# A sequence mixer and an MLP in one program: each y eviction on one engine, and a new hand-fixed order for every engine

## The chip, the cores and the metric

The program runs on one core of a Trainium2 chip. Its engines each work through a queue of their own: TensorE (PE, with the weight loads PEld), VectorE (DVE), ScalarE (ACT), GpSimd (POOL), and SyncE (SP), which here only issues transfers. The metric is the time of one execution on the device, in microseconds (us), lower is better.

## The reference

Two pre-normalised blocks with residuals. The first is a state-space mixer: k is convolved with four taps, multiplied by v, put through a long causal convolution along the sequence (an FFT of 4096 points in the reference) and multiplied by the normalised q. The second normalises again and runs two MLPs, the first of them with a shift of the four channel groups along the sequence.

```python
def _A_ref(q, k, v, shift_k, ssm_k, ssm_D):
    ...
    kv = k_shift * v
    kv_f = rfft(kv padded to 2S, along the sequence); kf_f = rfft(ssm_k padded to 2S)
    y = irfft(kv_f * kf_f)[:S]
    y = y + kv * ssm_D
    return q * y

x = A_q
h = x + _A_ref(_layernorm(x), A_k, A_v, A_shift_k, A_ssm_k, A_ssm_D)
n = _layernorm(h)
x1 = n + shifted(gelu(_layernorm(n) @ w1)) @ w2
h2 = h + x1 + gelu(_layernorm(x1) @ w3) @ w4
```

S is 2048, D is 512, the hidden width of the second MLP is 1792, all in bfloat16.

## The kernel before

The kernel does the long convolution as a sequence of small matrix products (a factored transform), with the 2048 positions laid out as 128 partitions by 16 tiles. Its work is first recorded as 926 operations (`Plan.add`), each with the keys it reads and writes, the engines that may do it and a cost in microseconds. None of these costs is used when the program is built: `Plan.issue` walks a string of numbers, `ISSUE`, and emits the operations in that order. Where an operation may run on more than one engine, the number carries a letter (V for DVE, A for ACT, G for POOL). So the order of every engine's queue, and the choice of engine, are fixed by `ISSUE`; each engine works strictly in that order, and waits that follow from the data are added by the framework.

Names used below, with the lines of the profile:

- Loads, all on SP: `k.0` to `k.3` (L240), `v.0` to `v.3` (L244), `h.0` to `h.3` (L249, the long filter), of 512 KB each; `q` as eight loads of 256 KB (L430), each of 64 of the 128 partitions. The statistics of four q tiles need two such loads.
- `psh` (L477): the four taps of k as 32 matmuls, `kvq` (L481, DVE) evicts them times v; eight of each (`kvq.0` to `kvq.3` for the first half of the channels, then again `kvq.0'` to `kvq.3'` for the second). `Rk` (L488): two transfers per `kvq` that bring the product to its next layout.
- `Rh` (L171 on ACT, L173 on DVE, 128x2048): the filter transposed by PE (`pt`, L502), four evictions. A first `tensor_tensor` on POOL must have added the skip term to the filter.
- Stage A: `pak` and `pah` (L518, eight matmuls each) for kv and the filter, 16 of each, evicted by `Tk` and `Th` (128x1024).
- Stage C: `pc` (L542 to L544), 32 products, evicted by `xt`; DVE multiplies the two spectra (`pr`, L674) and adds (L688, L690) in place.
- Stage G: `pg` (L744), 16, evicted by `Gs`. All of them must be done before the next stage, since the PSUM pools are exchanged there and each product of the next stage reads all of them.
- Last level: `py.0` to `py.7` (L797), each with two tiles of 512. The eviction `y` scales each of the two by a column of `rq` and adds 1 (L805 on ACT, L807 on DVE). `hs` (L812, DVE) multiplies the pair by the centred q; then statistics (L620, L621), a chain of ten small DVE operations for the reciprocal root (`rh`, L601 to L605 and L824 to L827), and the normalisation `hn` (L840 on ACT, L843 on DVE), four blocks of four tiles.
- The normalised tiles are transposed to `xT`: for blocks 0 and 1 by PE (`pt2`, L856) with an eviction on ACT, for blocks 2 and 3 by DMA transposes on SP (L900). `pw` (L868) is a product with w1 or w3, `gT` and `g2` its GELU on ACT (L872), `p2` (L945) the product with w2, evicted by `x1` (L951, DVE); `xn` is the second normalisation, `p4` (L1014) the product with w4, followed by the addition (L1019) and the stores.
- `qc` (L634 on ACT, L636 on DVE): q minus its mean, 16 tiles; `Wf'` (L173 and L588): four small copies of a table; `pv` (L880): matmuls on zeros which keep PE running.

A transfer takes one of eight completion semaphores in turn, so that the issue of one on SP waits for the landing of the eighth before it.

## Time and profile before

| | |
|---|---|
| median of 3 runs | 243.41 us (242.63 to 243.48) |
| the profiled execution | 243.34 us, of which the span from the first to the last instruction is 241.5 us |
| DVE, ACT and POOL busy | 161.0, 153.1 and 15.4 us |
| granted PE clock | 1.00 throughout |
| read from and written to memory | 13.11 MB and 2.10 MB |

The profile gives, for each engine, the instructions in order of time with the idle time ahead of them and what released it. A busy time of n instructions in a row overlaps by some 0.1 us at each boundary, so that durations of single instructions add up to more than the time from one start to the next.

### The profile page before, as it was taken

How to read it: one execution, taken by the hardware profiler on the slowest of the kernel's cores; microseconds unless marked ns; L12 is line 12 of the kernel's file. 1: busy time of each engine (PE TensorE's matmuls, PEld its weight loads, DVE VectorE, ACT ScalarE, POOL GpSimd, SP SyncE). 2: the span in 40 equal slices, each digit the busy share in tenths (PEclk: the TensorE clock that was granted, in tenths of full speed). 3: DMA queues.
4: the chain of work that ended last, by engine and by line, in shares of the span. 5: the costliest groups of instructions: out<-in, count | busy, mean ns of one | idle time of the engine just before them, and what ended most of it. 6: DMA issues, size and time to landing. Idle time of an engine off the chain costs nothing.

```text
span 241.5 us, 5031 instructions
## 1 busy us (share of the span) xinstructions
PE 224.7 (93%) x2069; PEld 147.6 (61%) x2069; DVE 161.0 (67%) x380; ACT 153.1 (63%) x205; POOL 15.4 (6%) x30
## 2 busy tenths in 40 slices
PE   8899987998899977999969999999999999999994
PEld 7899987897799864574434544444444444444454
DVE  6954999999999997999998899910440044004421
ACT  5788769999979998889657399763036204630000
POOL 2359300000000000000000000000000000000000
PEclk9999999999999999999999999999999999999999
DMA  6998876740000099100640025320002012001111
GB/s 218 391 374 203 168 187 213 174 91 3 0 3 0 20 343 390 39 0 0 88 84 5 1 53 99 61 52 3 10 22 54 0 24 65 0 0 42 46 43 45
DMA packets 22182, 21.82 MB, mean 90 GB/s; under 512 B 11916, under 2 KB 18704, under 8 KB 22160
## 3 DMA queue, kind: packets, MB, share of 16 engines
q1 hardware_dynamic: 21904, 21.37, 32.7%
q8 instruction: 16, 0.26, 0.5%
q10 hardware_dynamic: 256, 0.14, 0.2%
q14 instruction: 6, 0.05, 0.1%
HBM read 13.11 MB, written 2.10 MB: 63 GB/s over the span
## 4 chain that ended last, share of the span: by engine, by line
PE 51%; DVE 25%; DMA 12%; ACT 6%; issue 2%; SPq 1%; DVEq 0%; ACTq 0%
PE pw L868 23%; PE p L1014 20%; DVE kin L674 6%; DMA kin<-in_A_v_dram 5%; PE p L945 4%; DVE bst L620 4%; DVE ab L173 4%; ACT s L171 3%; DMA q_sb<-in_A_q_dram 3%; ACT ab L171 3%; DMA kin<-in_A_k_dram 2%; DVE ab L812 2%; DMA act<-ab 2%; DVE kin L688 1%; DVE bst L624 1%
## 5 line engine op out<-in xcount | busy, mean ns | idle before, releaser
L868 PE MATMUL pw<-act,wts 128*128 128x512 bf16 x288 | 64.0, 379 | 2.5 <-DMA act<-ab 1.9
L872 ACT ACTIVATE ab<-pw 128x512 bf16<-128x512 f32 x56 | 33.0, 596 | 38.4 <-PE pw L868 27.3
L1019 DVE TENSOR_TENSOR wts<-p,wts 128x1024 bf16<-128x1024 f32 (+2 forms) x10 | 10.1, 1012 | 62.0 <-PE p L1014 62.0
L868 PEld LDWEIGHTS <-wts 128*128 128x128 bf16 x288 | 28.0, 98 | 36.3 <-DMA act<-ab 2.4
L1014 PE MATMUL p<-wts,ab 128*128 128x512 bf16 (+1 forms) x238 | 48.9, 366 | 0.0
L1014 PEld LDWEIGHTS <-ab 128*128 128x128 bf16 x238 | 23.3, 98 | 25.3
L542 PE MATMUL pc<-ab,Wc 128*128 128x256 bf16 x128 | 30.7, 282 | 1.4 <-DVE ab L173 1.1
L171 ACT CAST s<-pc 128x1024 bf16<-128x1024 f32 x31 | 29.6, 1044 | 1.4 <-DVE kin L674 1.3
L544 PE MATMUL pc<-ab,Wc 128*128 128x128 bf16 x128 | 29.0, 227 | 0.0
L543 PE MATMUL pc<-ab,Wc 128*128 128x128 bf16 x128 | 28.0, 219 | 0.0
L543 PEld LDWEIGHTS <-Wc 128*128 128x128 bf16 x128 | 19.4, 151 | 1.4 <-issue 1.4
L674 DVE TENSOR_TENSOR kin<-s 128x2048 bf16<-128x2048 bf16 x16 | 19.4, 1221 | 0.6
L542 PEld LDWEIGHTS <-Wc 128*128 128x128 bf16 x128 | 19.4, 151 | 0.3
L544 PEld LDWEIGHTS <-Wc 128*128 128x128 bf16 x128 | 18.2, 142 | 0.0
L477 PE MATMUL psh<-ab 128*128 128x128 bf16 x256 | 15.6, 219 | 0.4 <-DVE kvq L481 0.4
L171 ACT CAST ab<-pah 128x1024 bf16<-128x1024 f32 x13 | 12.8, 1023 | 4.8 <-PE pah L518 4.8
L477 PEld LDWEIGHTS <-ab 128*128 128x128 bf16 x256 | 14.4, 98 | 0.9 <-issue 0.4
L945 PE MATMUL p<-wts,act 128*128 128x512 bf16 x64 | 15.0, 379 | 0.0
L481 DVE TENSOR_TENSOR kvq<-psh,kin 128x1024 bf16<-128x1024 f32 x8 | 9.7, 1218 | 4.8 <-DMA kin<-in_A_v_dram 4.8
L171 ACT CAST ab<-pak 128x1024 bf16<-128x1024 f32 x13 | 12.5, 1061 | 0.0
L951 DVE SCALAR_TENSOR_TENSOR s<-ab,rho,p 128x512 bf16<-128x512 bf16 x16 | 11.5, 739 | 1.2 <-PE p L945 1.1
L1000 DVE SCALAR_TENSOR_TENSOR wts<-s,mq,ab 128x512 f32<-128x512 bf16 x16 | 11.2, 749 | 0.2
(139 smaller groups left out, 316.3 us busy)
## 6 DMA issues: line engine op xcount, KB each, us to landing
wts<-in_B_w_dram SPq DMA_DIRECT2D x2, 1792.0 KB, 11.1
kin<-in_A_k_dram SPq DMA_DIRECT2D x4, 512.0 KB, 5.8
ab<-in_A_ssm_k_dram SPq DMA_DIRECT2D x4, 512.0 KB, 8.6
kin<-in_A_v_dram SPq DMA_DIRECT2D x4, 512.0 KB, 13.6
q_sb<-in_A_q_dram SPq DMA_DIRECT2D x8, 256.0 KB, 6.1
kin<-kvq SPq DMA_DIRECT2D x16, 128.0 KB, 5.1
out_dram<-wts SPq DMA_DIRECT2D x14, 128.0 KB, 2.3
Wc<-ab SPq DMA_DIRECT2D x4, 384.0 KB, 5.3
```

The source lines that it names most:

```text
L171: A.copy(o, src)
L477: T_.matmul(pv[:, g, i, :], lhsT=row(g, 4 * qr + i - j), rhs=dg()[:, 2 * g + cc, j, :], start=(j == 0), stop=(j == 3))
L542: T_.matmul(pv[:, kk], lhsT=W[0], rhs=T[:, :, 2 * k1:2 * k1 + 2, :], start=True, stop=False)
L543: T_.matmul(pv[:, kk, :, 0, :], lhsT=W[1], rhs=T[:, :, 2 * k1 + 1, :], start=False, stop=False)
L544: T_.matmul(pv[:, kk, :, 1, :], lhsT=W[2], rhs=T[:, :, 2 * k1, :], start=False, stop=True)
L674: v(1.13, lambda: V.tensor_tensor(out=prs(), in0=xs(0).unsqueeze(1).to_broadcast([P, 2, 2, 512]), in1=xs(1).unsqueeze(2).to_broadcast([P, ...
L868: T_.matmul(ps[:], lhsT=wt(w)[:, k, m * P:(m + 1) * P], rhs=xT()[:, k, 4 * b * P:(4 * b + 4) * P], start=(k == 0), stop=(k == DC - 1))
L872: add({"A": 0.49}, lambda: A.activation(dst(), X[pkey][:], ACT.Gelu_apprx_tanh), r + [pkey, "gelu"], [key])
L945: T_.matmul(ps[:, i, :], lhsT=gT()[:, m, t + i + 2 + off[m], :], rhs=wt("w2")[:, m, :], start=(m == 0), stop=(m == 3))
L951: v(0.66, lambda t=t, i=i, key=key: V.scalar_tensor_tensor(out=qn()[:, t + i, :], in0=hn()[:, t + i, :], scalar=rho[:, t + i:t + i + 1], i ...
L1000: v(0.66, lambda j=j, i=i, t=t + i: V.scalar_tensor_tensor(out=ofb()[:, j, i], in0=qn()[:, t, :], scalar=mq[:, t:t + 1], in1=hs()[:, t, :] ...
L1014: T_.matmul(ps[:, i, x0:x1], lhsT=g2(b % 2)[:, m, s0:s0 + P], rhs=wt("w4")[:, m, x0:x1], start=(m == 0), stop=(m == FC - 1))
```

## The change

Two things change in the code. First, the two halves of a y eviction, which were two operations with an engine each, become one operation on one engine; the key `("y", u % 4, i)` becomes `("y", u % 4)`. Second, several costs of the plan are altered (small DVE operations from 0.08 to 0.14, for example), and `ISSUE` is replaced as a whole. As the costs are not read when the program is built, all that reaches the chip is the new order, the new choice of engines and the pairing.

```diff
 ISSUE = """
-19 89 91 4 87 78 1 0 2 30 92 31 22 5 20 33 88 23 7 6 8 25 12 32 24 34V 42 35 41 40 43 48 93 10 26 90 28 29 95 15
...
+2 30 19 3 23 32 87 92 31 93 24 0 5 4 41 89 40 94 42 7 91 43 6 33 48 21 22 25 27 78 90 45 46 95 44 10 20 12 47
...
 """
...
             for i, f in enumerate(fns):
-                v(0.08, f, r if i == 0 else (), w, lat=0.24)
+                v(0.14, f, r if i == 0 else (), w, lat=0.22)
...
-        add({"A": 0.71, "V": 0.325}, centre, [("mq", t // 4), ("bst", t)], [("qc", t)])
+        add({"A": 0.69, "V": 0.27}, centre, [("mq", t // 4), ("bst", t)], [("qc", t)])
...
-        for i in range(2):
-            def scaled(e, i=i, t=2 * u + i):
+
+        def scaled(e):
+            for i in range(2):
+                t = 2 * u + i
                 if e == "A":
                     A.activation(ysb()[:, u % 4, i], X[key][:, i], ACT.Identity, bias=1.0, scale=rq[:, t:t + 1])
                 else:
                     V.tensor_scalar(ysb()[:, u % 4, i], X[key][:, i], rq[:, t:t + 1], 1.0, op0=MUL, op1=ADD)
-            add({"A": 0.53, "V": 0.6}, scaled, ["W", key, ("rq", 0)], [("y", u % 4, i)])
+
+        add({"A": 1.18, "V": 1.22}, scaled, ["W", key, ("rq", 0)], [("y", u % 4)])
```

Read from the two strings, the operations that changed their engine are:

| operation | before, DVE / ACT | after, DVE / ACT |
|---|---|---|
| `Rh` | 2 / 2 | 1 / 3 |
| `Th` and `Tk` | 3 / 13 each | 4 / 12 each |
| `Gs` | 6 / 10 | 5 / 11 |
| `Wf'` | 4 / 0 | 2 / 2 |
| `y` in halves | 1 / 15 | 2 / 14 |
| `hn` | 8 / 8 | 4 / 12 |
| `xn` | 4 / 12 | 6 / 10 |
| first step of one phase table (128x1024) | on DVE | on POOL |

The order on SP of the first transfers:

```
before: k3 k0 k2 k1 h2 h0 v0 h3 h1 v1 v2 q q v3 Rk Rk q q Rk Rk ...
after:  k3 k1 k2 k0 h0 h2 h1 v0 v3 v1 v2 h3 q Rk q q Rk q Rk Rk ...
```

From the first `psh` of the second channel half to stage C, PE's queue holds:

```
before: psh1' pah5 pah15 psh0' pah13 psh2' pah6 pak4 pak5 pak2 pah11 pak6 pak1 psh3' pak0 pah12 pak7 pak3 pah1 pah10 pah9 pah8 | pc
after:  psh0' pah1 pah9 psh3' pah13 pak6 pak2 pak1 pah3 pak7 pak4 psh1' pak3 pak5 psh2' pah14 pak0 pah12 pah15 pah10 | pc
```

After the last `Gs`, ACT's queue begins with:

```
before: qc12 y0b qc14 y1 y2 y3 y4 y5 y7a hn1 hn2 xT0 y6 xT2 hn7 y7b gT xT6 gT gT xT4 hn8 gT hn11 gT gT gT gT
after:  qc3 qc12 qc15 y0 qc13 y2 y3 y5 y4 hn3 hn1 hn2 y7 hn0 xT2 y6 xT0 hn5 hn6 hn7 xT4 gT gT xT6 gT gT hn11 gT hn10 gT gT gT
```

and DVE's:

```
before: y0a hs0 ... rh block 0 between hs2 hs3 and four statistics ... hn0 hn3 ... hn6 hn4 hn5 ... hs7 hs6 ... hn10 ... hn9
after:  y1 hs1 ... rh block 0 with only hs2 between ... hn4 ... rh block 2, hn9 hs7 hs6, hn8
```

## The prediction

> **What bounds the kernel now.** The table by stages comes first; its cuts are places where the chain of waits changes hands. Columns: stretch, then busy time of PE, PEld, DVE, ACT and POOL, the clock, the DMA share and GB/s.

> ```profile
> 27.00:46.40 19.40, 16.84 (x316) 15.42 (x314) 18.94 (x30) 16.08 (x19) 0.00 (x0) 1.00 0.68 178
> 46.40:93.10 46.70, 41.61 (x564) 39.36 (x561) 45.69 (x67) 45.05 (x50) 0.00 (x0) 1.00 0.31 88
> 93.10:118.40 25.30, 23.31 (x216) 13.72 (x217) 23.20 (x86) 21.96 (x34) 0.00 (x0) 1.00 0.22 76
> 118.40:122.70 4.30, 2.44 (x12) 0.88 (x9) 4.06 (x19) 1.52 (x2) 0.00 (x0) 1.00 0.84 95
> 122.70:238.04 115.34, 115.33 (x566) 54.38 (x567) 50.44 (x139) 48.07 (x79) 0.00 (x0) 1.00 0.16 34
> ```

> The last row is closed: from 122.70 PE works 115.33 of 115.34 us, and the change removes no product there. So the question is when that stretch begins. The chain in order of time (start, us, what) shows its entry:

> ```profile
> 91.99 1.14 DVE ab L173
> ...
> 93.27 0.85 PE py L797 x6
> 94.28 0.70 ACT wts L805
> ...
> 117.08 0.58 DVE bst L620
> ...
> 118.08 0.32 DVE ab L843
> ...
> 118.45 4.22 DMA act<-ab
> ...
> 122.71 3.63 PE pw L868 x16
> ```

> The last Gs is evicted at 93.1 by DVE, PE starts the last level at 93.27, and the first `pw` of block 2 starts at 122.71, released by a DMA transpose. Two intervals can move: the time to 93.27, in which DVE (45.69) and ACT (45.05) both fill 46.70 us, and the 29.44 us from 93.27 to 122.71, in which DVE leads (23.20 against 21.96).

> Ahead of that the loads set the pace; DVE in order of time, with the idle time before each in brackets:

> ```profile
> 14.51 1.23 DVE L481 TENSOR_TENSOR kvq<-psh,kin 128x1024 bf16<-128x1024 f32 x1 [1.53 <-DMA kin<-in_A_v_dram]
> ...
> 19.63 1.23 DVE L481 TENSOR_TENSOR kvq<-psh,kin 128x1024 bf16<-128x1024 f32 x1 [2.30 <-DMA kin<-in_A_v_dram]
> 21.83 1.22 DVE L481 TENSOR_TENSOR kvq<-psh,kin 128x1024 bf16<-128x1024 f32 x1 [0.97 <-DMA kin<-in_A_v_dram]
> 23.98 2.47 DVE L624 BATCH_NORM_STATS2 bst<-q_sb 128x6 f32<-128x512 bf16 x4 [0.93 <-DMA q_sb<-in_A_q_dram]
> ...
> 26.89 0.62 DVE L636 TENSOR_SCALAR q_sb<-q_sb,mq 128x512 bf16<-128x512 bf16 x2
> ...
> 28.56 1.22 DVE L481 TENSOR_TENSOR kvq<-psh,kin 128x1024 bf16<-128x1024 f32 x1
> ```

> These are arrivals by place in SP's queue: the 7th load (v0) at 14.5, the 10th (v1) at 19.6, the 11th (v2) at 21.8, the 12th and 13th (a q pair) at 24.0; v3, the 14th, is used at 28.56. The rate halves at about 17:

> ```profile
> 10.00:17.00 7.00, 7.00 (x125) 6.83 (x122) 5.06 (x7) 6.40 (x6) 2.46 (x5) 1.00 1.03 415
> 17.00:26.00 9.00, 8.76 (x156) 8.20 (x154) 4.80 (x7) 6.88 (x8) 8.90 (x11) 1.00 0.95 208
> ```

> That is 1.3 us for 512 KB at 415 GB/s and 2.5 at 208.

> **The change part by part.** *1. The first transfers.* After the change all v are 8th to 11th, h3 moves from 8th to 12th, and the first q pair from 12th and 13th to 13th and 15th, with an Rk between. The v side gains: `kvq3` need not wait for 28.56; it runs second, at about 17. The q side loses: 512 KB and an Rk more lie ahead of its first pair. If the half rate holds as before, that is 24.0 + 2.5 + 0.6 = 27.1. If the rate stayed at 415, the five loads after the 7th (v0, v3, v1, v2, h3) end at 14.5 + 5 x 1.3 = 21.0, and two half loads and the Rk bring it to 22.9. I take 25.5: the slow stretch began when the first q loads came up, and these come up later now, so v is likely served at the fast rate and q at the slow one. DVE waits for this pair once `kvq0` to `kvq3` and `Rh` are done, at 22 to 23.

> *2. To stage C.* PE's queue from the first second-half `psh`:

> ```profile
> 30.32 1.96 PE L477 MATMUL psh<-ab 128*128 128x128 bf16 x32
> ...
> 44.21 0.33 PE L542 MATMUL pc<-ab,Wc 128*128 128x256 bf16 x1
> ```

> Before, four `psh` and 18 stage-A groups fill 13.9 us. After, it is four and 16, and the first, `psh0'`, needs the PSUM buffer that DVE's `Th0` frees. `Th0` stands behind the q pair: 25.5 + 2.47 (statistics) + 0.44 (means, from there to 26.89 before) + 3 x 0.31 (centrings) + 1.14 (the eviction, as at 91.99) = 30.5. So the block begins when it began before, and the bounds for `pc` are 44.2 and, with another 1.5 of waits, 45.7. I take 45.4, since `psh1'`, `psh2'` and `pah15` now each wait for an eviction that stands late on its engine (`Tk1`, `Tk4`, `kvq2'`). The first `xt` on ACT follows 1.2 later, at 46.6.

> *3. Stages C and G.* ACT's rows:

> ```profile
> 46.39 3.82 ACT L171 CAST s<-pc 128x1024 bf16<-128x1024 f32 x4
> ...
> 71.99 7.57 ACT L171 CAST s<-pc 128x1024 bf16<-128x1024 f32 x8 [1.33 <-DVE kin L674]
> ...
> 88.17 4.84 ACT L171 CAST ab<-pg 128x1024 bf16<-128x1024 f32 x5 [0.15 <-PE pg L744]
> ...
> 10.60 2.84 ACT L171 COPY ab<-pk 128x1024 bf16<-128x1024 bf16 x3 [1.40 <-PE pk L452]
> ```

> One eviction costs (7.57 - 0.1) / 8 = 0.93 back to back. Before, ACT does 48 from 46.39 to 93.01: 44.6 of work and 2.0 of waits. After, the order gives it 49 (31 `xt`, 2 `Th`, 5 `Tk`, 11 `Gs`) and two `Wf'`, for which the nearest row is the 2.84 of three copies, 0.92 each: 47.4. The waits lie between 0.3 and the old 2.0; I take 1.1, so 48.5. DVE sheds in the same stretch a `Gs`, two `Wf'` and some small operations and gains a `Tk` and an `xt`: about 0.5 less than before. Its 45 us end inside ACT's. So the last `Gs` is now ACT's, at 46.6 + 48.5 = 95.1, and `py` starts at 95.25, against 93.27: +2.0.

> *4. Last level to block 2.* The edit that names the change:

> ```profile
> 95.00 0.75 DVE L807 TENSOR_SCALAR wts<-py,rq 128x512 bf16<-128x512 f32 x1 [1.62 <-ACT wts L805]
> ...
> 94.86 0.71 ACT L634 ACTIVATE q_sb<-q_sb,mq 128x512 bf16<-128x512 bf16 x1
> 98.44 3.67 ACT L805 ACTIVATE wts<-py,rq 128x512 bf16<-128x512 f32 x6 [0.28 <-PE py L797]
> ...
> 104.26 1.52 ACT L840 ACTIVATE ab<-ab,nb,rh 128x512 bf16<-128x512 bf16 x2 [0.74 <-DVE nb L827]
> 105.85 1.01 ACT L171 COPY act<-pt 128x1024 bf16<-128x1024 bf16 x1
> 115.56 1.60 ACT L872 ACTIVATE act<-pw 128x512 bf16<-128x512 f32 x3
> 117.42 0.60 ACT L872 ACTIVATE act<-pw 128x512 bf16<-128x512 f32 x1 [0.27 <-PE pw L868]
> ...
> 114.50 5.22 SPq L900 DMA_TRANSPOSE act<-ab  x4
> ...
> act<-ab SPq DMA_TRANSPOSE x8, 2.5
> ...
> 118.72 0.17 DVE L603 SCALAR_TENSOR_TENSOR nwt<-rh 128x8 f32<-128x8 f32 x1
> 118.92 0.17 DVE L604 TENSOR_TENSOR nwt<-nwt,vh 128x8 f32<-128x8 f32 x1
> ```

> DVE's half of y0 waited for ACT's half and started 0.72 after it (95.00 against 94.28). That wait goes, but DVE now does two halves of y1, 0.7 more, and `hs` starts as late as before: nothing gained. The small chain costs 0.20 a step when nothing stands between (118.72 to 118.92). In the new order `rh` 0 has only `hs2` between its steps: about 1 us of DVE lost there, and the result earlier. DVE also sheds four `hn`, 0.32 each, and has three statistics of block 3 (0.58 each) less ahead of its last `hn` of block 2. That one ended 25.1 after `py` began (118.08 + 0.32 - 93.27); now it should end at 25.1 - 1.3 - 1.8 + 1.0 = 23.0.

> What is late next is ACT. From the barrier to the last GELU of block 1 it has four `qc` (0.71 each), seven y pairs (1.22), nine `hn` (0.76), four `xT` (1.01) and eight GELUs (0.53): 2.8 + 8.5 + 6.8 + 4.0 + 4.3 = 26.4, or about 25.0 if neighbours overlap by 0.1. As it must also wait for the first `py`, I take 25.9. Before, the same point came at 24.7 (118.02) with pauses. Then the two `p2` (16 matmuls, 3.5), which earlier ran beside the transposes, stand ahead of `pw` of block 2: 25.9 + 3.5 = 29.4 after `py`, where 29.44 stood. The transposes end earlier: `hn10` stands three GELUs ahead, at 24.3; one issue is 1.3 (5.22 for four), a landing 2.5, so 28.1. So the old wait for the DMA is exchanged for one for ACT: -0.1. A `pv` of 0.2 leaves the closed stretch: -0.2.

> [...]

> **The sum.**

> ```profile
> span 241.5 us, 5031 instructions
> 238.04 0.42 DVE wts L1019
> ```

> The profiled execution took 243.34, 1.8 around its span; the median of the runs, 243.41, is 0.07 above. 243.34 + 2.0 - 0.1 - 0.2 = 245.0.

> **The rivals.**

> *Not slower: the loads stay fast.* If 415 GB/s holds past 17, the q pair lands at 22.9. Of these 2.6 I give `pc` 2.0, since ACT's stage-A evictions stand in the way: 243.0. For it: the slow stretch is also the one in which POOL fills its time (8.90 of 9.00). Against it: the rows give no fast q.

> *Faster: the shift to ACT pays.* DVE ends the third stretch now, and ACT is 3.3 us short of full in it. If ACT's operations fit into its pauses, DVE's `hn8` at 23.0 decides: half an issue ahead of it (0.6) and 2.5 to land give `pw` at 26.1, against 29.4: 245.0 - 3.3 = 241.7. Against it: the sum of 25.0 leaves ACT no pause. [...]

> *Slower still.* q at 27.1 (+1.6), ACT waiting 2.0 as before (+0.9): 247.5.

> *The named edit does nothing* is part of the forecast: the wait of 1.62 goes and no time with it. The new order decides.

> **How the numbers follow.** Forecast 45%, fast loads 20%, offload pays 15%, slower still 20%. About 0.5%, 1.2 us, is what a measurement of this kernel can tell from no change. Faster (under 242.2) is the offload: 0.15. Within are the fast loads and the low edge of the forecast (0.05): 0.25. Slower is the rest: 0.60. The range is 242.0 to 247.6, which leaves out most of the offload case and the edge of the last; the forecast's own is 244 to 246.3.

> **What would show it.** Step 1: DVE's first statistics on q start at 25 to 26, after the four `kvq`. Step 2: `pc` starts at 45 to 46. Step 3: the last `Gs` ends on ACT at about 95, ACT having no pause over 1. Step 4: no wait of DVE for ACT at y1; DVE waiting for ACT in the third stretch; PE entering `pw` of block 2 from `p2` without a DMA wait. The forecast is wrong if DVE still ends that stretch, or if q lands before 24.

## The result, and the profile after

| | before | after |
|---|---|---|
| median of the runs, us | 243.40 (242.38 to 244.37, 15 runs) | 245.33 (243.03 to 246.49, 15 runs) |
| ratio, 95% interval | 1 | 1.0063 (1.0035 to 1.0090) |
| profiled execution, us | 243.34, span 241.5 | 244.43, span 242.6 |
| mean granted TensorE clock of it | 1.000 | 0.993 |

The changed kernel is slower by 0.6%. In all tables and runs below a median is over all runs of a kernel, while a ratio leaves out runs over 1.5% above the fastest of the same kernel (four of the kernel with two `hn` back on DVE, one of that with the three-fold fill).

The stages of the profiled execution, cut at the same events as before (first `xt` on ACT, last `Gs`, last GELU of block 1, first `pw` of block 2); columns as in the prediction's first table:

```profile
27.00:47.90 20.90, 17.17 (x301) 15.96 (x300) 18.95 (x33) 15.89 (x17) 0.00 (x0) 0.92 0.65 168
47.90:95.60 47.70, 43.23 (x588) 41.10 (x586) 44.73 (x61) 47.55 (x52) 0.00 (x0) 1.00 0.30 88
95.60:121.25 25.65, 23.28 (x220) 13.60 (x223) 24.23 (x87) 24.75 (x39) 0.00 (x0) 1.00 0.22 63
121.25:123.84 2.59, 2.59 (x12) 1.15 (x12) 2.42 (x13) 1.16 (x2) 0.00 (x0) 1.00 0.61 91
123.84:239.13 115.29, 114.74 (x553) 54.09 (x562) 51.51 (x143) 47.13 (x78) 0.00 (x0) 1.00 0.17 36
```

The closed stretch begins 1.1 us later (123.84 against 122.71) and is as long as it was (115.29 against 115.34). So all that happened lies ahead of it, and the row that differs most is the first: its clock is 0.92, where every row of before has 1.00. The rows of DVE and then of PE show where, each in order of time (start, us, engine and line, operation; in brackets the idle time before and what ended it; `...` where rows are left out):

```profile
25.56 2.47 DVE L624 BATCH_NORM_STATS2 bst<-q_sb 128x6 f32<-128x512 bf16 x4 [2.16 <-DMA q_sb<-in_A_q_dram]
...
29.27 1.22 DVE L173 CAST ab<-pah 128x1024 bf16<-128x1024 f32 x1
...
28.09 0.46 PE L518 MATMUL pah<-WA,s 64*128 64x128 bf16 x8
30.54 2.94 PE L477 MATMUL psh<-ab 128*128 128x128 bf16 x32 [1.99 <-DVE ab L173]
33.42 1.07 PE L518 MATMUL pah<-WA,s 64*128 64x128 bf16 x16
34.42 2.07 PE L477 MATMUL psh<-ab 128*128 128x128 bf16 x32
...
46.75 0.27 PE L542 MATMUL pc<-ab,Wc 128*128 128x256 bf16 x1 [0.40 <-ACT ab L171]
...
95.67 0.41 PE L797 MATMUL py<-ab,Wf 128*64 128x512 bf16 x2 [0.70 <-DVE nwt L604]
...
123.84 3.62 PE L871 MATMUL pw<-act,wts 128*128 128x512 bf16 x16
```

The q pair reaches DVE at 25.56, `Th0` runs at 29.27 behind it, and PE, which had ended `pah6` at 28.55, starts `psh0'` at 30.54 after a pause of 1.99 us. Up to here it is the forecast, step by step. What the forecast did not have is the next number: these 32 matmuls take 2.94 us, where 32 took 1.96 before, and the 16 of `pah` behind them 1.07 instead of 0.72. The table in stretches of 3.41 us, cut where the granted clock changes, shows why:

```profile
24.44:27.85 3.41, 3.41 (x64) 3.28 (x64) 2.29 (x4) 3.41 (x4) 2.35 (x3) 1.00 1.06 223
27.85:31.27 3.42, 1.43 (x28) 1.32 (x27) 3.32 (x9) 3.04 (x3) 0.00 (x0) 1.00 0.84 202
31.27:34.68 3.41, 3.41 (x41) 3.04 (x39) 3.09 (x7) 0.57 (x1) 0.00 (x0) 0.50 1.06 279
34.68:38.09 3.41, 3.00 (x65) 2.82 (x64) 2.15 (x6) 2.52 (x4) 0.00 (x0) 1.00 1.12 312
```

The clock is halved for exactly one stretch of 3.41 us, from 31.27, right behind a stretch in which PE was busy for 1.43 of 3.42 us. The time from `psh0'` to `pc` grows to 16.2 us by it, and `pc` starts at 46.75, 2.5 later than before. From there to the first `py` both kernels need the same: 48.92 us after, 49.06 before.

The third stretch became shorter, 28.17 us from `py` to `pw` of block 2 against 29.44. Its chain of waits (start, us, what), which ran on DVE and ended in a DMA, now runs on ACT and ends on PE:

```profile
94.39 1.14 DVE ab L173
...
95.67 1.05 PE py L797 x8
...
103.80 1.27 ACT wts L807 x2
...
119.76 1.47 ACT act L875 x3
121.25 2.75 PE p L948 x12
124.00 1.08 PE pw L871 x5
```

Over the 15 runs the clock and the time go together:

| mean granted clock of a run | runs | us |
|---|---|---|
| 0.998 to 1.000 | 3 | 243.03, 243.05, 243.38 |
| 0.992 or 0.993 | 11 | 244.34 to 246.03, median 245.34 |
| 0.986 | 1 | 246.49 |

One stretch of 3.41 us at half clock in a span of 243 is a mean of 0.993, two are 0.986. The three runs without one have the time of the kernel before. That kernel kept its clock: in the 86 runs of it that were timed beside the experiments the mean is never under 0.998.

### The profile page after: what moved, and what is told of

It reads as the page before. It is cut to its first block, busy times and chain, and to the rows that moved or that the text cites. A ratio compares the mean times of both kernels' runs of the same rounds, so it can differ in the third digit from the quotient of the medians.

```text
span 242.6 us, 5026 instructions
## 1 busy us (share of the span) xinstructions
PE 225.1 (93%) x2057; PEld 148.5 (61%) x2069; DVE 160.1 (66%) x376; ACT 156.1 (64%) x208; POOL 17.8 (7%) x31
## 4 chain that ended last, share of the span: by engine, by line
PE 61%; ACT 15%; DVE 10%; DMA 9%; issue 3%; SPq 0%; ACTq 0%; DVEq 0%
PE pw L871 22%; PE p L1017 20%; PE p L948 6%; ACT s L171 5%; DMA kin<-in_A_v_dram 4%; PE psh L477 4%; ACT ab L171 3%; DMA q_sb<-in_A_q_dram 3%; PE pc L542 3%; DVE kin L674 2%; ACT ab L843 2%; DVE ab L173 2%; PE py L797 2%; DMA kin<-in_A_k_dram 2%; ACT act L875 2%
## 5 line engine op out<-in xcount | busy, mean ns | idle before, releaser
L1017 PEld LDWEIGHTS <-ab 128*128 128x128 bf16 x238 | 23.3, 98 | 25.3
L542 PE MATMUL pc<-ab,Wc 128*128 128x256 bf16 x128 | 31.0, 283 | 1.2 <-ACT ab L171 0.7
L171 ACT CAST s<-pc 128x1024 bf16<-128x1024 f32 x31 | 29.5, 1060 | 0.3 <-PE pc L544 0.3
L674 DVE TENSOR_TENSOR kin<-s 128x2048 bf16<-128x2048 bf16 x16 | 19.2, 1221 | 2.3 <-ACT s L171 1.9
L542 PEld LDWEIGHTS <-Wc 128*128 128x128 bf16 x128 | 19.3, 151 | 0.4
L477 PE MATMUL psh<-ab 128*128 128x128 bf16 x256 | 16.4, 227 | 2.1 <-DVE ab L173 2.0
L477 PEld LDWEIGHTS <-ab 128*128 128x128 bf16 x256 | 15.5, 102 | 2.5 <-issue 2.1
L171 ACT CAST ab<-pah 128x1024 bf16<-128x1024 f32 x12 | 11.8, 1022 | 6.9 <-PE pah L518 6.9
L948 PE MATMUL p<-wts,act 128*128 128x512 bf16 x63 | 14.9, 379 | 0.1
L481 DVE TENSOR_TENSOR kvq<-psh,kin 128x1024 bf16<-128x1024 f32 x8 | 9.8, 1225 | 4.7 <-DMA kin<-in_A_v_dram 2.2
L171 ACT CAST ab<-pak 128x1024 bf16<-128x1024 f32 x12 | 11.8, 1054 | 0.0
L624 DVE BATCH_NORM_STATS2 bst<-q_sb 128x6 f32<-128x512 bf16 x16 | 10.2, 681 | 2.2 <-DMA q_sb<-in_A_q_dram 2.2
```

Source lines behind the costliest of these rows:

```text
L171: A.copy(o, src)
L477: T_.matmul(pv[:, g, i, :], lhsT=row(g, 4 * qr + i - j), rhs=dg()[:, 2 * g + cc, j, :], start=(j == 0), stop=(j == 3))
L542: T_.matmul(pv[:, kk], lhsT=W[0], rhs=T[:, :, 2 * k1:2 * k1 + 2, :], start=True, stop=False)
L624: v(0.615, lambda t=t: V.bn_stats(bst[:, t, :], X["q_sb"][:, t, :]), [("q", 0, t // 4), ("q", 1, t // 4)], [("bst", t)], lat=0.12)
L674: v(1.18, lambda: V.tensor_tensor(out=prs(), in0=xs(0).unsqueeze(1).to_broadcast([P, 2, 2, 512]), in1=xs(1).unsqueeze(2).to_broadcast([P, ...
L948: T_.matmul(ps[:, i, :], lhsT=gT()[:, m, t + i + 2 + off[m], :], rhs=wt("w2")[:, m, :], start=(m == 0), stop=(m == 3))
```

## The experiments

"Clock" is the mean granted clock of a run; line numbers in the rows of these kernels are up to three off those of before. Each kernel was timed against the kernel before on the same chip in five rounds.

### Keeping PE busy in the pause

In `stage_a` of the kernel after:

```
-            for ee in range(4):
+            for ee in [x for _ in range(6 if (w, i) == (1, 6) else 1) for x in range(4)]:
```

> Kernel after, one thing changed: the eight matmuls of pah6 are issued six times, into the same place with the same values, so that PE is busy in the pause of 2.0 us ahead of psh0'. Clock theory (the pause of 28.6 to 30.5 makes the clock drop to half for 3.4 us, and this is most of the loss): granted clock 1.000, psh0' takes 1.96 instead of 2.94, pc starts near 45.7, time 243.2 to 243.8, ratio to before 0.999 to 1.002. Rival (the forecast as it stood: late q loads and more ACT work, the clock adds little): the clock is 1.000, but DVE and ACT still set the start of pc and of the last level, time 244.7 to 245.5.

243.02 us (242.23 to 244.20, 12 runs), ratio 1.0002 (0.9980 to 1.0025), clock 0.998 or more in all 12. PE in order of time:

```profile
28.18 1.76 PE L517 MATMUL pah<-WA,s 64*128 64x128 bf16 x48
29.88 1.96 PE L476 MATMUL psh<-ab 128*128 128x128 bf16 x32
...
44.66 0.27 PE L541 MATMUL pc<-ab,Wc 128*128 128x256 bf16 x1 [0.40 <-ACT ab L170]
...
93.52 0.41 PE L796 MATMUL py<-ab,Wf 128*64 128x512 bf16 x2 [0.70 <-DVE nwt L603]
...
121.69 3.62 PE L870 MATMUL pw<-act,wts 128*128 128x512 bf16 x16
```

The added matmuls compute nothing new, and PE still cannot start `psh0'` before `Th0`. Yet `pc` starts 14.78 us after `psh0'` instead of 16.21, at 44.66, and the loss is gone: what cost time was the half clock behind the pause, not the wait. The q pair came 0.66 earlier in this execution (`psh0'` at 29.88), which is the rest of the 2.1 us at `pc`. The first `py` is back at 93.52 (93.27 before), and what is left of the new order is the shorter third stretch: `pw` of block 2 at 121.69, 28.17 behind it. This profiled execution, 242.29 us, is one of the fastest of the twelve; their median shows the loss gone and no gain.

With three issues instead of six:

> The kernel after, with the eight matmuls of pah6 issued three times instead of six: the pause of 2.0 us shrinks by two times 0.35 to 1.3, and the least busy 3.41 us around it rise from 0.42 to about 0.62 busy. If what drops the clock is a window less than about half busy: no drop, 243.0 (242.3 to 243.6), as with six. If any pause of more than about 1 us drops it: drops in most runs, 244.5 to 245.5. Something between (drops in few runs, median 243.3 to 244) would put the limit near 0.6.

243.33 us (241.86 to 245.80, 12 runs), ratio 1.0010 (0.9982 to 1.0038). Eight runs have a clock of 0.998 or more (241.86 to 243.66), four 0.991 or less (244.06 to 245.80): the answer in between, with a drop in a third of the runs instead of 12 in 15.

### Taking `Th0` away from the q pair

`Th0`, evicted by DVE behind the q pair, is given to ACT behind `Th2`:

```
-DVE: ... qc6 qc7 qc4 Th0 | second q pair ...      ACT: ... Th2 Rh Rh Th6 ...
+DVE: ... qc6 qc7 qc4 | second q pair ...          ACT: ... Th2 Th0 Rh Rh Th6 ...
```

> Kernel after, the eviction Th0 moved from DVE, where it stands behind the statistics of the first q pair, to ACT behind Th2. Clock theory: PE's pause ahead of psh0' shrinks under 0.5 us, the clock stays 1.000, and as ACT's idle 3.1 us in this place are also used, pc starts at 44 to 45.5 and the time is 242.3 to 243.6. Rival (the q loads set DVE's pace, whatever PE does): pc moves under 0.5 us, time 244.7 to 245.5.

245.73 us (243.46 to 246.67, 8 runs), ratio 1.0092 (1.0055 to 1.0130); a clock under 0.994 in five of the eight. The 242.3 to 243.6 of the clock theory did not come. PE:

```profile
28.47 1.96 PE L476 MATMUL psh<-ab 128*128 128x128 bf16 x32
...
32.85 1.95 PE L476 MATMUL psh<-ab 128*128 128x128 bf16 x32 [1.52 <-DVE kvq L480]
```

`psh0'` starts at once, and the pause, now 1.52 us, stands at the next `psh`: it waits for `kvq0'`, which is behind the second q pair on DVE. The profiled execution, 243.50, kept its clock until PE's work was done; the runs above 245 did not.

The other remedy leaves `Th0` on DVE and takes both out of the way:

```
-DVE: st st st st mean qc6 qc7 qc4 Th0 | st st st st mean kvq0' ...
+DVE: st st Th0 st st mean qc6 qc7 qc4 kvq0' | st st st st mean ...
```

> The kernel after, with two changes of VectorE's order alone: Th0 goes between the second and the third statistics of the first q pair instead of behind the whole pair, and the eviction kvq of head 0's second half goes ahead of the second q pair instead of behind it. Theory (the loss is the 2.0 us pause of TensorE, which takes the granted clock to half for 3.41 us, and the pause comes only from Th0 standing behind the q pair): the second half's shift of head 0 starts 28.6 instead of 30.54, no pause over 1 us is left between 27 and 46, the clock is 1.00 in every run, pc starts at 43.5 to 44.5, py at 92.5 to 93.5, and the time is 242.0 (241.3 to 242.8), below both kernels. Rival (the q pairs as a whole make VectorE late, the place of Th0 only decides where TensorE waits): the pause comes back behind, at the third or fourth shift, 1.5 us or more, the clock drops in half of the runs, and the time is 244.5 to 245.5.

244.56 us (244.17 to 245.77, 6 runs), ratio 1.0072 (1.0047 to 1.0098), and a lower clock in all six, although in the profiled execution no pause of PE over 0.9 us is left. The expected 242.0 is refuted, and so is the plain form of the theory behind it, that it takes a long pause. The stretch ahead of the drop and the one with it:

```profile
23.12:26.53 3.41, 2.61 (x46) 2.40 (x47) 0.30 (x1) 3.34 (x5) 2.40 (x4) 1.00 1.01 213
26.53:29.94 3.41, 3.27 (x52) 2.85 (x50) 2.77 (x4) 2.75 (x2) 1.37 (x2) 0.50 0.80 172
```

PE was busy for 2.61 of 3.41 us, and the clock was halved all the same. This drop also lies ahead of the place that was edited: the first operation that moved, `Th0`, runs on DVE at 28.37, and up to 26.53 every queue is that of the kernel after. So the run shows a second weak place, in a part that both kernels share; whether the edit mends the first one it does not show, and only one of its six runs was profiled.

In the kernel before, and in one execution with the three-fold fill, PE was busy for less, and the clock stayed (first the row of before, then that of the other kernel):

```profile
35.09:38.51 3.42, 2.33 (x57) 2.01 (x58) 3.38 (x6) 3.00 (x4) 0.00 (x0) 1.00 1.10 316
```

```profile
30.26:33.67 3.41, 2.38 (x47) 2.28 (x47) 3.38 (x6) 1.05 (x2) 0.00 (x0) 1.00 1.04 224
```

So the busy time alone did not decide here. What fills these stretches differs by its shape: in the first it is mostly the transposes `pt`, with 128\*64 in their rows, in the other two `pah`, `pak` and `psh`, with 64\*128 and 128\*128. The second of these numbers is here called the columns. Counted by columns the 2.61 us are 0.48 of the stretch, and the row of before stays at 0.68. Counted so, with each matmul's time weighted by its columns, the stretches ahead of the drop in the five profiled executions that had one ahead of `pc` were between 0.33 and 0.49 full (about 0.38 in the kernel after). That is a reading and no rule, for two stretches inside this range kept the clock: in the kernel before the wait for its transposes leaves PE 1.53 us busy in the 3.41 us from 120.42, 0.45, and in the kernel of "A pause that did not come" with the fill the 3.41 us from 93.64, with PE busy for 2.18, most of it `py` on 64 columns, come to 0.39. Nor did transposes alone lower the clock: in the kernel before they fill all of the 3.41 us from 21.44, and it stayed at 1.00.

One more fill should then mend that kernel: `pah2` twice, ahead of the transposes, `range(2 if (w, i) == (1, 2) else 1)` in the line of the first experiment.

> The kernel of the run with Th0 early (after, with Th0 inside the first q pair and kvq ahead of the second), which had no pause of TensorE over 0.9 us and yet a lower clock in 6 of 6 runs; here the eight matmuls of pah2 are issued twice, which fills 0.35 of the 0.44 us that TensorE waits ahead of the second block of transposes. In the run without the fill the 3.41 us ahead of the drop (23.12 to 26.53) were 0.76 busy, most of it with transposes, which use 64 of the 128 columns (0.48, counted by columns). If the busy share counted by columns sets the clock, the window rises to about 0.57: no drop in most runs, 242.5 (241.8 to 243.2). If TensorE's order, and not its idle time, does it in another way, or the window is set by the later loads, the drops stay in most runs: 244.6 (244.1 to 245.3).

244.08 us (242.67 to 245.25, 12 runs), ratio 1.0034 (1.0009 to 1.0058). Four runs kept the clock (242.67 to 243.14), eight did not (243.54 to 245.25). In the profiled one the first weak stretch was no longer followed by a drop, but a later one was:

```profile
35.24:38.65 3.41, 1.69 (x33) 1.50 (x33) 3.41 (x7) 2.56 (x4) 0.00 (x0) 1.00 1.11 283
38.65:42.07 3.42, 3.42 (x42) 3.22 (x39) 2.77 (x4) 1.28 (x3) 0.00 (x0) 0.50 0.33 85
```

There PE waits for `kvq` and two evictions behind the second q pair. Both ends of the expectation came true in part. Four of twelve runs against none of six are too few to show that this fill helped; the run says no more than that the lateness of VectorE's order has several places to come out.

### The named edit alone

The kernel before, with both halves of y0 on DVE, one behind the other; the pair also moved ahead of `qc13`, which had stood ahead of it:

```
-DVE: ... qc13 y0a hs0 ...        ACT: ... qc12 y0b qc14 ...
+DVE: ... y0b y0a qc13 hs0 ...    ACT: ... qc12 qc14 ...
```

> Kernel before, only both halves of y0 on DVE, one behind the other (the named edit where it mattered, with the old order). Forecast's step 4 (nothing gained: the wait of 1.62 goes, DVE does 0.7 more): py to hs0 stays 2.4 to 2.6 us, ratio to before 0.998 to 1.002. Rival (the wait was on the path and is worth its 0.7): hs0 starts 0.7 earlier and the time falls by 0.5 to 0.8, ratio 0.997 to 0.998.

243.47 us (242.04 to 243.98, 12 runs), ratio 1.0000 (0.9979 to 1.0021). DVE at `y0`, first in the kernel before, then here:

```profile
95.78 0.69 DVE L812 TENSOR_TENSOR ab<-wts,q_sb 128x1024 bf16<-128x1024 bf16 x1
```

```profile
94.88 1.41 DVE L806 TENSOR_SCALAR wts<-py,rq 128x512 bf16<-128x512 f32 x2 [1.19 <-PE py L796]
...
96.46 0.68 DVE L811 TENSOR_TENSOR ab<-wts,q_sb 128x1024 bf16<-128x1024 bf16 x1
```

In before the first py starts at 93.27 and `hs0` 2.51 us later; here 93.83 and 2.63. The wait for ACT has become a second half on DVE. `qc13`, which now stands between, takes 0.26 of the 2.63 (from 96.20 to 96.46), so the pairing by itself may be worth some 0.1 us; the times, 0.2% either way, do not show it.

### Two `hn` back on DVE

The kernel after, with `hn10` and `hn11` taken from ACT and put behind `hn9` on DVE.

> Kernel after, hn10 and hn11 moved back from ACT to DVE behind hn9. If ACT sets the end of the third stretch as forecast: from py to the first pw of block 2 the time falls by 1.0 to 1.5 us (two hn of 0.76), total 0.8 to 1.5 below the kernel after, ratio 1.000 to 1.003. Rival (DMA transposes or p2 take over at once): that stretch stays within 0.4 us of 28.3, ratio 1.005 to 1.008.

244.71 us (242.26 to 246.39, 12 runs), ratio 1.0023 (0.9992 to 1.0055). The two medians, 244.71 and 243.17 of the kernel before, give 1.0063, as the kernel after has it; eight of the twelve runs have a clock under 0.994. So the times do not say that the move helped, and the trace decides. PE:

```profile
111.61 1.02 PE L870 MATMUL pw<-act,wts 128*128 128x512 bf16 x4 [1.46 <-ACT act L170]
...
119.96 3.62 PE L947 MATMUL p<-wts,act 128*128 128x512 bf16 x16
123.41 3.62 PE L870 MATMUL pw<-act,wts 128*128 128x512 bf16 x16
```

From the first `py` (95.23) to `pw` of block 2 it is 28.18 us, as in the kernel after (28.17); 1.0 to 1.5 less was expected of a bound by ACT. With these two gone from ACT, PE goes from the first `pw` on without a gap to speak of and ends at the same time: ACT's last GELU and PE's own work stand level there.

A second try, with four `hn` moved, was made on the kernel of the next section:

> The order old ahead of py and new behind it, and four normalisations hn of ScalarE moved to VectorE: hn1, hn2 in their place and hn10, hn11 directly behind hn9. If ScalarE sets the first pw, as the chain of waits of after has it (ScalarE busy from 103.8 to 111.95 but for 0.3): ScalarE is 1.4 us shorter ahead of its copies, VectorE 0.6 longer, the first pw is 15.0 to 15.6 after py instead of 16.37, the pw of block 2 27.0 to 27.6 after py unless its transposes hold it, and the time is 241.5 (240.8 to 242.3). If VectorE or the transposes set it, the pw of block 2 stays at 28.2 to 29.0 and the time at 242.4.

251.56 us (250.46 to 251.97, 5 runs), ratio 1.0341 (1.0310 to 1.0372). Neither case. DVE, then PE:

```profile
111.18 0.73 DVE L845 TENSOR_SCALAR ab<-ab,rh,nb 128x512 bf16<-128x512 bf16 x2
...
111.97 1.04 PE L858 MATMUL pt<-ident,ab 128*128 128x128 bf16 x8 [8.71 <-DVE ab L845]
...
118.07 1.02 PE L870 MATMUL pw<-act,wts 128*128 128x512 bf16 x3 [1.10 <-ACT act L170]
```

`hn1` and `hn2` had stood in the one written order behind the statistics of the next group, which cost nothing as long as ACT did them. On DVE they waited for those statistics, PE's transposes of block 0 waited 8.71 us for them, the first `pw` came 25.99 us after `py` instead of 16.37, and the clock was at 0.50 from 105.53 to 115.77. The run tells of a badly chosen place, and nothing of what bounds ACT.

### Half the order each

Two kernels join the orders at the first `py`: the old one up to it and the new one behind, and the reverse. Each has the engines and the y evictions that belong to its second part.

```
first:   [before's order up to py] + [after's order of all that is left]
second:  [after's order up to py] + [before's order of all that is left]
```

> The old order and engines of the kernel before for everything ahead of the first py, and the new order, engines and y evictions of the kernel after for all that follows. Theory (the new order loses ahead of py, through the granted clock, and gains behind it): the first py at 93.3 (92.3 to 94.0 with what the loads vary), clock 1.00 in all runs, from py to the pw of block 2 28.2 to 29.0 instead of 29.44, the closed stretch 115.3, and the time 242.4 (241.6 to 243.0), ratio 0.996. Rival (the shorter third stretch of after is only what the late py gives to the transposes, which land at a fixed time): pw of block 2 again waits 1.5 us or more for its transposes, and the time is 243.3 as before.

> The other way round: the new order and engines ahead of the first py, the old order, engines and y halves behind it. Theory: the clock falls in most runs (mean 0.993), py at 95.7, py to the pw of block 2 29.4, closed stretch 115.3, and the time is 246.0 (245.2 to 246.8), slower than after itself by the 1.2 us that the new order gains behind py. Rival (the new order's loss lies behind py): 243.3.

The first: 242.75 us (241.66 to 243.56, 12 runs), ratio 0.9976 (0.9958 to 0.9994), clock 0.998 or more in all. The second: 246.38 us (243.64 to 247.19, 9 runs), ratio 1.0111 (1.0072 to 1.0150), clock under 0.994 in seven of nine; the two that kept it took 243.64 and 243.72. PE of the first, then of the second:

```profile
93.78 0.41 PE L796 MATMUL py<-ab,Wf 128*64 128x512 bf16 x2 [0.84 <-DVE ab L172]
...
110.16 1.02 PE L870 MATMUL pw<-act,wts 128*128 128x512 bf16 x3 [1.47 <-ACT act L170]
...
122.93 3.63 PE L870 MATMUL pw<-act,wts 128*128 128x512 bf16 x16 [0.80 <-DMA act<-ab]
```

```profile
31.25 3.04 PE L476 MATMUL psh<-ab 128*128 128x128 bf16 x32 [2.25 <-DVE ab L172]
...
96.35 0.62 PE L796 MATMUL py<-ab,Wf 128*64 128x512 bf16 x4 [0.70 <-DVE nwt L603]
...
112.23 1.02 PE L867 MATMUL pw<-act,wts 128*128 128x512 bf16 x3 [0.35 <-ACT act L170]
...
125.86 3.63 PE L867 MATMUL pw<-act,wts 128*128 128x512 bf16 x16 [1.78 <-DMA act<-ab]
```

The loss stands ahead of `py` and a gain behind it. From `py` to `pw` of block 2 the old order takes 29.44 us (before) and 29.51 (the second kernel), with a DMA wait of 1.8 to 1.9 us in it; the new order takes 28.17 (after), and 29.15 in the first kernel, where 0.80 of the wait came back. So its gain in these executions is between 0.3 and 1.3 us, by when the transposes land, and the first kernel, 242.75, is the only one here whose interval lies below the kernel before.

How long a transpose took to land counted as much as the order here. In the kernel before the fourth is issued 25.18 us after `py` and lands 4.22 later. In the kernel with the fill of the next section, which has the old order behind `py`, it is issued at the same 25.18, and `pw` of block 2 starts 27.70 after `py` without a wait, 2.52 behind that issue (one of 0.48 follows at 128.39). So the 1.27 us by which the two profiled executions differ are not a fixed price of the old order; what is shown for the new second half is the 0.24% of the runs.

### A pause that did not come

The kernel before, with VectorE's order changed so that `kvq1'` stands behind the q pair (`... st st st kvq1' st mean kvq0' qc ...` becomes `... st st st st mean qc qc kvq1' kvq0' ...`), without and with a fill of six times `pah13`:

> The kernel before, with a pause of TensorE made by VectorE's order: the eviction kvq of head 1's second half goes behind the last statistics, the mean and two normalisations of the q pair that stood partly behind it, so that the fourth shift, which waits for its PSUM buffer, starts at about 34.7 instead of 33.12, some 2.0 us after TensorE's last matmul. Clock theory: the granted clock falls to half for 3.41 us in most runs (mean 0.993), and those runs are 1.5 to 2 us slower than the runs without it: median 245.0 (244.3 to 245.7). Rival one, the pause costs nothing but its length and this is absorbed before pc: 243.4 (243.0 to 243.9), clock 1.00 in all runs. Rival two, its length goes to the end whole: 244.9 with the clock at 1.00.

> The kernel of the run before it (the kernel before with a pause made by VectorE's order), and the eight matmuls of the pah that stands in the pause issued six times, which fill about 1.75 us of it. Clock theory: clock 1.00 in all runs, 243.5 (243.0 to 244.0). Rival two (the length of the wait goes to the end): 244.9 as without the fill, since the fourth shift starts no earlier.

243.26 us (241.65 to 244.62, 12 runs), ratio 0.9995 (0.9973 to 1.0018), and 243.19 (242.70 to 244.50, 12 runs), ratio 1.0020 (1.0001 to 1.0040). The clock was 0.998 or more in all runs but one with the fill (0.992, 244.50, its slowest). The first tells nothing of the theory, since the pause did not arise:

```profile
29.82 1.96 PE L476 MATMUL psh<-ab 128*128 128x128 bf16 x32
...
32.10 1.96 PE L476 MATMUL psh<-ab 128*128 128x128 bf16 x32
```

The second q pair was there at 29.04 in this execution (30.06 in before's), so that `kvq1'` was not late, and PE had no idle time over 0.9 us.

## Why the forecast of 245.0 was right, and where it was not

*The time.* 245.33 was measured where 245.0 was predicted. The sum holds errors of opposite sign, a half clock that it did not contain and two terms that were too large. The forecast had the late q pair and the pause of PE behind it right, but not what the pause did: without the half clock its other terms, as measured below, come to about -0.4 us, and the kernel with the fill is not slower (1.0002). So the direction came true through a cost that the forecast did not name, and that the number came within 0.3 us is luck.

*Step 1, the q pair.* 25.5 was predicted and 25.56 seen, behind the four `kvq`. In the seven other kernels with the same order of loads it came between 24.90 and 27.17, so the upper bound, 27.1, was met and the lower, 22.9, was never near.

*Step 2, to stage C.* The pause and its end were right (`psh0'` at 30.5; 30.54). "I take 45.4" for `pc` failed, with 46.75, by the half clock. Where the clock is kept, the predicted 14.9 us from `psh0'` to `pc` are right: 14.78 with the fill. After, they are 16.21; the 32 matmuls of `psh0'` are 0.98 longer, the 16 behind them 0.35, the next 32 0.11: 1.44. The premise that failed is unspoken: that PE's rows keep their length. The table of stages of before shows 1.00 in its clock column throughout, and the forecast took that as a property of the chip and not of the order.

*Step 3, stages C and G.* The term "the waits lie between 0.3 and the old 2.0; I take 1.1" was too large. In the row 47.90:95.60 ACT is busy for 47.55 of 47.70 us (47.4 predicted), so 0.15 is left for waits. The last `Gs` ended on DVE after all, at 95.53 (predicted on ACT, 95.1). `py` came 2.40 later than before instead of 2.0: 2.54 from `pc`, less 0.14.

*Step 4, behind `py`.* That the named edit gives nothing that the times can tell is shown by the run that makes it with the old order. `hn8` ended 22.96 after `py` (predicted 23.0) and the last GELU of block 1 25.54 after it (25.9):

```profile
118.23 0.40 DVE L846 TENSOR_SCALAR ab<-ab,rh,nb 128x512 bf16<-128x512 bf16 x1
...
119.56 1.65 ACT L875 ACTIVATE act<-pw 128x512 bf16<-128x512 f32 x3
```

"Then the two `p2` (16 matmuls, 3.5) ... stand ahead: 25.9 + 3.5" was too long. In the chain above, 12 of the 16 follow the last GELU, 2.75 us; the first four need only the earlier ones and had run. So `pw` of block 2 stands 28.17 after `py` and not 29.4, and the gain of this stretch is 1.27 and not 0.1. There is no DMA wait ahead of it, as predicted; the exchange of the DMA for ACT is what the chain shows, though PE itself goes from `pw` into `p2` without a gap, so that its own work ends the stretch as much as ACT. Three other kernels with this second half have a DMA wait there, of 0.25, 0.64 and 0.80.

*The closed stretch* gave 0.05 and not the 0.2 of one `pv`: 115.29 against 115.34, and about 115.3 in the other kernels but one: with the fill of "A pause that did not come" it is 116.0, with a DMA wait inside it.

*The sum with what was measured:* +2.40 (to `py`) - 1.27 - 0.05 = +1.1, which is the difference of the two profiled executions (244.43 - 243.34). Of the 2.40, 1.44 are the half clock. The median moved by 1.9 since ten of the 15 runs lie above the profiled one; what makes those longer no trace shows.

*The rivals.* "Not slower: the loads stay fast" was wrong in its reason, as q came at 25.56. But the time that it gave, 243.0, is that of the three runs that kept their clock (243.03 to 243.38) and of the kernel with the fill (243.02), for another reason: the late start costs little when the clock stays, and the third stretch gives it back. "The shift to ACT pays" was right in part, since the new order is better behind `py`; DVE's `hn8` at 23.0 did not decide, PE and ACT did. With the old first half it is worth 0.24% (0.06 to 0.42). "Slower still", 247.5, did not come: q at 27.1 is possible, as said, but ACT's waits were 0.15 and not 2.0, and the slowest run took 246.49.

*What stays open.* By what measure a stretch counts as too little was not settled. By busy time a stretch of 0.76 lost the clock and one of 0.45 kept it; by columns one of 0.49 lost it and one of 0.39 kept it. Counted by rows and columns together (`pah` and `pak`, 64\*128, then count half as well) the stretch of before from 35.09 comes to 0.34 and kept it, that of the kernel with `Th0` early to about 0.38 and lost it. A direct test, the same busy time with full and with half-width matmuls, was not made.

## What to carry to other kernels

Here a new order halved the TensorE clock for 3.41 us behind a pause of 1.99 us, and with `Th0` early behind 0.8 us of idle time in 3.41, so the clock column of the stages is to be read for every version, and the time of each run beside its clock; matmuls that compute nothing new, put into such a pause, are a cheap test. In the kernel after six times the product of one place were a full remedy (0.998 or more in 12 of 12 runs) and three times a partial one (in 8 of 12); in the kernel with `Th0` early, where several places are weak, one fill left eight of twelve runs with a drop. When an order is searched as a whole, its halves can be worth opposite amounts: joined at a place that all work must pass, they can be measured one by one, and the better one kept. An operation that changes its engine may also need a new place in the order: two `hn` that stood behind the next group's statistics held PE for 8.71 us on DVE, and the first `pw` came 25.99 us after `py` instead of the 16.37 with them on ACT.

## What the runs showed of the hardware that was not expected

In the kernel with `Th0` early the granted clock fell to 0.50 for 3.41 us behind a stretch in which PE was idle for only 0.8 us of 3.41 (row 23.12:26.53), most of its work transposes with 128\*64 in their rows. It kept 1.00 behind stretches with 1.09 us of idle time (before, row 35.09:38.51) and 1.03 (three-fold fill, row 30.26:33.67) among matmuls with 64\*128 or 128\*128 in theirs, and behind one with 1.88 us (before, from 120.42). Runs of the kernel after with one drop took 2.3 us longer than those without (median of the 11 runs with one drop, 245.34, less the middle one of the three without, 243.05). In the profiled execution 1.44 of that are matmuls at half speed; whether the drop causes the rest too, or loads that came late in the same runs, is not shown.
